# New due dates for a planned attention and feed-forward kernel, with odd-sized tiles moved into the pool of constants

## The chip, the core and the metric

The kernel runs on one core of a Trainium2 chip. The metric is the device time of one execution in microseconds. Three executions of the kernel before took 598.49, 599.57 and 600.98 us; their median, 599.57 us, is what the changed kernel is compared with.

## The reference

Local attention with a few global keys and a distance bias, and then a feed-forward block with a sigmoid gate. Batch 4, 8 heads, 768 positions, head width 64; 3,072 tokens of width 512 go through weights of 512 x 2048 and 2048 x 512.

```python
scores = scale * np.matmul(q, k.transpose(0, 1, 3, 2)) - slopes * dist   # 8 heads
scores = np.where(is_global | is_local, scores, -1000000000.0)           # 8 global keys, 96 local ones
a = np.exp(scores - np.max(scores, axis=-1, keepdims=True))
a = a / (np.sum(a, axis=-1, keepdims=True) + 1e-09)
x = np.matmul(a, v)                  # to (3072, 512)
h = x @ w_in                         # (3072, 2048)
out = (h * (1.0 / (1.0 + np.exp(-1.702 * h)))) @ w_out
```

## The kernel before

The work is cut into 24 blocks of 128 query rows and 12 chunks of two blocks. The four blocks that are the first of their batch are done in `first` with keys and queries turned by TensorE; every other block goes through `prep` (load of q, k and v into `raw`, split into two 16-bit halves, a transposing DMA into `QK`), four calls of `unit` (two heads each: `scores`, `rows` into a tile `p`, exponentials in place, halves into `hl`, a transposing DMA into `pt`, `values` into `pv`) and `finish` (weighing, halves into `x16`, a transposing DMA into `xT`). The weights are split in `weights` in 16 pieces. The feed-forward block of the first three chunks runs over eight steps each with `up` and `down`; from chunk 3 on `up_two` and `down_two` work on two steps at once with a scheme of seven products in place of eight.

Nothing is ordered by the compiler. Each piece of work is a `Task` with a cost in us for each engine that may run it (`on`), the tasks it waits for (`after`), the tiles it uses (`bufs`) and a wanted time. `Work.order` works out due dates backward along the dependences, adds to each task `NUDGE[tag]`, the correction that is written down for the name (`wk.tag`) of its piece, and then plays the plan through: an engine that is free takes, of the tasks that are ready and whose tiles are free, the one with the earliest due date. The instructions are emitted in that order, and each engine and the SP queue keep to it on the chip. A task isn't taken before `early()`, which is 24 us before its due date, or at `soon` where that is set. Pieces with the tag "" have no correction.

Nearly all DMAs are issued on SP's queue, in the plan's order: a DMA whose data isn't there yet holds up all that stand behind it. The plan charges a load of q, k or v 1.35 us, a transpose into `pt` 1.4 us, one into `QK` 2.8 us.

Tiles come from rings: `Ring` has a name, a number of buffers and whether its order is `loose`. `Buf()` gives the tile. `r_hl.tiles` are fixed tiles of the pool `const`; all others are allocated in the pool `sb` behind `const`, in the order of their first use. By the sizes in the code the tiles in `sb` of the kernel before begin between 64 and 416 bytes past a multiple of 512 bytes, and `hl` 416 bytes past one; none begins at a multiple. So `raw` and `t` stand at 160, `QK`, `VR` and `g` at 352, `x16` at 224.

Behind the main work stands a verdict on whether the fast way's assumptions held. Its inputs are sums and maxima that are gathered on the way (`checks`), among them second readings of the weights: 32 pieces `ws..again` of 512 KB that borrow the two buffers of the ring `wa`, each with one instruction of ScalarE (line 1024) and one of VectorE (line 1026), and of q, k and v of four blocks (`again`). The verdict has three tasks: `rows_hold` on VectorE, one small matmul (line 1072) on TensorE, and `all_hold` on VectorE, which writes `flag`. All engines then load `flag` and branch over the function `general`, a slow general version that isn't run here.

```python
    for c in range(2, NCHUNK):
        for s in range(NST):
            start[c, s] = t_
            t_ += PACE if c < TWO else PACE2
    v1 = add({"DVE": 2.4}, rows_hold, [covers, *checks])
    v2 = add({"PE": 0.1}, lambda e: nc.tensor.matmul(pb()[0:1, 0:3], ones, fin, start=True, stop=True), [v1], [pb])
    add({"DVE": 1.2}, all_hold, [v2], [pb], 575.0)
    redo = nc.values_load(flag[0:1, 0:1], min_val=0, max_val=1)
    with tc.If(redo > 0):
```

The last product of the kernel is piece `down113` (chunk 11, steps 6 and 7), wanted at `start[11, 6] + LAG`. With T0 = 20, 16 steps of 6 us, eight of 5.9 us (chunk 2) and 70 of 5.7 us, `start[11, 6]` is 562.2 us; LAG is 16, and the second half of the rows is wanted 2.6 us later. Its last output leaves by a DMA on ScalarE's queue (line 935).

Of the kernel before, what the change touches and what calls it, by code (L numbers as in the profile page):

```python
# [1 line left out]

# [6 lines left out]
F32 = mybir.dt.float32  # L9
F32R = mybir.dt.float32r  # L10
F16 = mybir.dt.float16
# [8 lines left out]
P = 128  # L20
NG = 32
# [5 lines left out]

NUDGE = {"T0": -15.8, "T1": -14.5, "T2": 7.5, "T3": 23.9, "block0": -14.5, "block1": -12.1, "block10": 7.2, "block11": 28.4,  # L30
# [27 lines left out]

NG = 8
SKIP = 24  # L60
# [18 lines left out]
        self.tiles = None  # L79


class Buf:


# [5 lines left out]

    def __call__(self):
        if self.ring.tiles:
            return self.view(self.ring.tiles[self.i % self.ring.bufs])
        if self.t is None:
            self.t = self.ring.pool.tile(self.shape, self.dtype, tag=self.ring.tag, name=self.name, bufs=self.ring.bufs)
        return self.t
# [14 lines left out]
class Work:  # L111
# [5 lines left out]
    def add(self, on, fn, after=(), bufs=(), want=1e9):  # L117
        t = Task(on, fn, [a for a in after if a is not None], bufs, want)
        t.tag = self.tag
        for a in t.after:  # L120
            a.next.append(t)
        for b in t.bufs:
            b.users.append(t)
        self.tasks.append(t)
        return t

    def order(self):
# [18 lines left out]
        for t in self.tasks:  # L146
            t.due += NUDGE.get(t.tag, 0.0)
        free = dict.fromkeys(("PE", "DVE", "ACT", "POOL", "SP"), 0.0)
# [84 lines left out]
def kernel(  # L233
# [12 lines left out]
    B, H, S, D = q.shape  # L246
# [11 lines left out]
    const = ctx.enter_context(tc.tile_pool(name="const", bufs=1))  # L258
# [31 lines left out]
    def ring(tag, bufs, pool=sb, loose=False):  # L290
        return Ring(pool, tag, bufs, loose, pool is ps)

    r_raw, r_qk16, r_QK, r_KG = ring("raw", 2), ring("qk16", 1), ring("QK", 3), ring("KG", 1)
    r_VR, r_VG, r_sm = ring("VR", 4), ring("VG", 1), ring("sm", 3)
    r_pr, r_hl, r_pt = ring("pr", 2), ring("hl", 2), ring("pt", 4)
    r_hl.tiles = [const.tile([P, 8 * P], F16, name=f"hl{j}") for j in range(2)]
    r_VF = ring("VF", 3, loose=True)
    r_x, r_x16, r_xT, r_xS = ring("x", 1), ring("x16", 1), ring("xT", 2), ring("xS", 2)
    r_ws, r_wa = ring("ws", 3), ring("wa", 2, loose=True)
    r_t, r_g = ring("t", 3, loose=True), ring("g", 3, loose=True)  # L300
# [5 lines left out]
    wk = Work()  # L306
# [115 lines left out]
    def load(n, raw, parts=(0, 1, 2)):  # L422
        b, i = place(n)
        return [add({"SP": 1.35}, lambda e, z=z: nc.sync.dma_start(
            raw()[:, z], (q, k, v)[z][b, :, i * P:(i + 1) * P, :].rearrange("h p d -> p h d")), bufs=[raw]) for z in parts]
# [525 lines left out]
    T0, PACE0, PACE, PACE2, LAG, SKEW, LEAD = 20.0, 6.0, 5.9, 5.7, 16.0, 3, 68.0  # L951
# [42 lines left out]
    whole = seq + [(c, s) for c in range(2, TWO) for s in range(NST)]  # L994
# [15 lines left out]
            down_two(c, S, start[c, 2 * S] + LAG)  # L1010
    wk.tag = ""
    for n in range(EARLY):
        raw = Buf(r_raw, [P, 3, H, D], F32, f"again{n}")
        ld = load(n, raw)
        guard(n, raw, ld, 440.0 + 30 * n)
        for t in ld:
            t.soon = 400.0 + 30 * n
    for s in range(NST):
        for u in range(2):
            for half in range(2):  # L1020
                ws = Buf(r_wa, [P, 512, 2], I32, f"ws{s}_{u}{half}again")
                t0 = add({"SP": 1.6}, lambda e, s=s, u=u, ws=ws, half=half: load_weights(nc, ws(), w_in, w_out, s, u, half), bufs=[ws])
                o, hi_w = 2 * (2 * s + u) + half, lambda ws=ws: ws()[:, :, 1].bitcast(F32)
                t1 = add({"ACT": 0.64}, lambda e, o=o, hi_w=hi_w: nc.scalar.activation(
                    hi_w(), hi_w(), AF.Square, accum_out=e2[:, 0, o:o + 1]), [t0], [ws])
                checks.append(add({"DVE": 0.6}, lambda e, o=o, hi_w=hi_w: nc.vector.tensor_reduce(
                    e2[:, 1, o:o + 1], hi_w(), axis=AX.X, op=ALU.min), [t1], [ws], 275.0 + 8.0 * o))
                t0.soon = 265.0 + 8.0 * o
# [9 lines left out]
    ones = const.tile([P, 1], F32, name="ones")  # L1038
    nc.gpsimd.memset(ones, 1.0)
    pb = Buf(r_h, [P, 512], F32, "pb")  # L1040

    def rows_hold(e):
        nc.vector.tensor_scalar(NM[:, 0:EARLY], top, 1.0 / SC, None, ALU.mult)
# [17 lines left out]
    def all_hold(e):  # L1061
# [6 lines left out]
            nc.vector.scalar_tensor_tensor(tot[:, 0:1], o_, 1.0, tot[:, 0:1], ALU.is_lt, ALU.add)  # L1068
        nc.vector.tensor_scalar(flag, tot[:, 0:1], 1.0, None, ALU.min)

    v1 = add({"DVE": 2.4}, rows_hold, [covers, *checks])
    v2 = add({"PE": 0.1}, lambda e: nc.tensor.matmul(pb()[0:1, 0:3], ones, fin, start=True, stop=True), [v1], [pb])
    add({"DVE": 1.2}, all_hold, [v2], [pb], 575.0)
# [215 lines left out]
```

## Time and profile before

| | before |
|---|---|
| median of 3 runs | 599.57 us (598.49 to 600.98) |
| profiled execution, its time | 598.66 us |
| its span, first to last instruction | 596.8 us |
| TensorE busy (matmuls) | 576.2 us, 97% |
| VectorE busy | 492.8 us, 83% |
| ScalarE busy | 460.4 us, 77% |
| granted TensorE clock, mean | 0.997 |
| SP's data queue, share of 16 engines' span | 87.8% |

Busy time of TensorE is the time in which a matmul was under way; its idle time is what is left of the span. The device time of the execution is 1.9 us longer than its span. Instructions of sequencers (loads of a register, branches, waits) don't count as busy.

### The profile page before, as it was taken

How to read it: one execution, taken by the hardware profiler on the slowest of the kernel's cores; microseconds unless marked ns; L12 is line 12 of the kernel's file. 1: busy time of each engine (PE TensorE's matmuls, PEld its weight loads, DVE VectorE, ACT ScalarE, POOL GpSimd, SP SyncE). 2: the span in 40 equal slices, each digit the busy share in tenths (PEclk: the TensorE clock that was granted, in tenths of full speed). 3: DMA queues.
4: the chain of work that ended last, by engine and by line, in shares of the span. 5: the costliest groups of instructions: out<-in, count | busy, mean ns of one | idle time of the engine just before them, and what ended most of it. 6: DMA issues, size and time to landing. Idle time of an engine off the chain costs nothing.

```text
span 596.8 us, 16959 instructions
## 1 busy us (share of the span) xinstructions
PE 576.2 (97%) x6774; PEld 432.5 (72%) x6776; DVE 492.8 (83%) x1164; ACT 460.4 (77%) x1091; POOL 1.6 (0%) x10
## 2 busy tenths in 40 slices
PE   8899999999999999999999999998999999999994
PEld 5787676777686668767677768767866875887893
DVE  5899999998999998887699889877969779776541
ACT  4688798998669888988579789858987897874441
POOL 1000000000000000000000000000000000000000
PEclk9999999999999999999999999999999999999998
DMA  8998999998996877799799999999998999971001
GB/s 223 315 307 242 269 233 243 190 201 171 177 153 118 151 152 162 146 186 204 170 230 197 199 197 190 222 191 192 217 222 197 210 202 174 251 143 36 20 1 41
DMA packets 268502, 109.58 MB, mean 184 GB/s; under 512 B 249536, under 2 KB 250048, under 8 KB 268416
## 3 DMA queue, kind: packets, MB, share of 16 engines
q1 hardware_dynamic: 267984, 108.30, 87.8%
q8 instruction: 54, 0.88, 0.7%
q14 instruction: 32, 0.26, 0.1%
q10 hardware_dynamic: 432, 0.13, 0.1%
HBM read 57.67 MB, written 6.29 MB: 107 GB/s over the span
## 4 chain that ended last, share of the span: by engine, by line
PE 58%; DVE 16%; DMA 10%; ACT 9%; issue 3%; SPq 2%; DVEq 0%; ACTq 0%
PE y L917 27%; PE pa L849 13%; PE pb L849 10%; PE s L556 3%; DMA raw<-in_q_dram 3%; ACT p L572 2%; DVE w L399 2%; DVE wa L396 2%; DMA ws_01again<-in_moe_w_in_dram 2%; DMA raw<-in_k_dram 2%; DMA QK<-QK 2%; DVE p L562 1%; ACT junk L431 1%; DVE hl L577 1%; PE h L809 1%
## 5 line engine op out<-in xcount | busy, mean ns | idle before, releaser
L917 PE MATMUL y<-w,g 128*128 128x512 f16 (+1 forms) x1248 | 265.1, 363 | 0.9 <-DVE g L890 0.9
L917 PEld LDWEIGHTS <-g 128*128 128x128 f16 x1248 | 118.0, 98 | 106.5 <-DVE g L890 1.4
L849 PEld LDWEIGHTS <-w 128*128 128x128 f16 x1728 | 100.8, 98 | 5.1 <-DVE t L882 0.7
L572 ACT ACTIVATE p<-p,NM 128x232 f32<-128x232 f32 x160 | 76.6, 481 | 9.2 <-DVE NM L562 9.0
L849 PEld LDWEIGHTS <-T 128*128 128x128 f16 x1296 | 76.8, 98 | 6.3 <-issue 0.8
L809 PE MATMUL h<-xT,w 128*128 128x256 f16 x576 | 68.3, 273 | 0.7 <-DVE t L819 0.7
L562 DVE CUSTOM_DVE_ANT_0 p<-s,mm 128x232 f32<-128x232 f32 x160 | 58.2, 395 | 6.0 <-PE s L556 4.9
L809 PEld LDWEIGHTS <-w 128*128 128x128 f16 x576 | 55.3, 98 | 9.4 <-issue 1.2
L577 DVE TENSOR_TENSOR hl<-p,hl 128x464 f16<-128x464 f32 x80 | 50.9, 637 | 11.2 <-ACT hl L576 10.9
L890 DVE SCALAR_TENSOR_TENSOR g<-t,g 128x512 f16<-128x512 f32 x72 | 48.9, 688 | 7.6 <-ACT g L889 7.1
L857 DVE TENSOR_TENSOR h<-pb,h 128x256 f32<-128x256 f32 x72 | 29.2, 419 | 26.6 <-PE pb L849 21.1
L889 ACT ACTIVATE g<-t 128x512 f16<-128x512 f32 x72 | 44.7, 627 | 7.4 <-DVE t L882 5.8
L881 ACT ACTIVATE t<-h 128x512 f32<-128x512 f32 (+1 forms) x72 | 36.3, 517 | 17.5 <-DVE h L857 15.9
L576 ACT CAST hl<-p 128x464 f16<-128x464 f32 x80 | 46.1, 576 | 3.6 <-DMA pt<-hl 2.0
L849 PE MATMUL pa<-xS,T 128*128 128x128 f16 x648 | 45.0, 220 | 0.7 <-ACT h L865 0.7
L882 DVE SCALAR_TENSOR_TENSOR t<-t,h 128x512 f32<-128x512 f32 x72 | 38.5, 553 | 5.9 <-ACT t L881 5.9
L556 PEld LDWEIGHTS <-QK 128*128 128x128 f16 x640 | 36.3, 98 | 6.9 <-DVE NM L562 2.1
L556 PE MATMUL s<-QK 128*128 128x128 f16 x320 | 38.5, 219 | 0.5 <-DMA QK<-QK 0.5
L849 PE MATMUL pb<-xS,w 128*128 128x128 f16 x540 | 37.2, 219 | 0.4 <-ACT h L854 0.4
L849 PE MATMUL pa<-xT,w 128*128 128x128 f16 x540 | 36.9, 220 | 0.5 <-DVE t L882 0.5
L587 PE MATMUL pv<-VR,pt 128*128 128x64 f16 x288 | 34.1, 194 | 2.6 <-DMA pt<-hl 2.6
L588 PE MATMUL pv<-VR,pt 128*128 128x64 f16 x288 | 34.1, 194 | 0.0
(178 smaller groups left out, 1004.3 us busy)
## 6 DMA issues: line engine op xcount, KB each, us to landing
ws<-in_moe_w_in_dram SPq DMA_DIRECT2D x8, 1024.0 KB
ws<-in_moe_w_out_dram SPq DMA_DIRECT2D x8, 1024.0 KB
raw<-in_q_dram SPq DMA_DIRECT2D x24, 256.0 KB
raw<-in_k_dram SPq DMA_DIRECT2D x24, 256.0 KB
out_dram<-yo SPq DMA_DIRECT2D x22, 256.0 KB
raw<-in_v_dram SPq DMA_DIRECT2D x20, 256.0 KB
QK<-QK SPq DMA_DIRECT2D x40, 128.0 KB
ws_00again<-in_moe_w_in_dram SPq DMA_DIRECT2D x8, 512.0 KB
```

Of the source, the lines that this page charges most:

```text
L556: nc.tensor.matmul(sp()[:, j, lo:hi], d["QK"]()[:, 0, h, :], K[:, 1 + z, h, P - (hi - lo):], start=(z == 0), stop=(z == 1), skip_group_che ...
L562: nc.vector.tensor_tensor_reduce(out=pr()[:, j, :], in0=sp()[:, j, :], in1=m, scale=-1.0 / SC, scalar=3.0e38, op0=ALU.add, op1=ALU.min, ac ...
L572: ex.append(add({"ACT": 0.473}, lambda e, j=j: nc.scalar.activation(pr()[:, j, :], pr()[:, j, :], AF.Exp, bias=NM[:, n, hs[j]:hs[j] + 1], ...
L576: t4 = add({"ACT": 0.5}, lambda e: nc.scalar.copy(hl()[:, 0, :, SKIP:], pr()), ex, [pr, hl])
L577: t5 = add({"DVE": 0.55}, lambda e: nc.vector.tensor_sub(hl()[:, 1, :, SKIP:], pr(), hl()[:, 0, :, SKIP:]), [t4], [pr, hl])
L809: nc.tensor.matmul(ph()[:, fi, :], w1(s, cc, z, fi), X[:, y, cc, :], start=(j + cc == 0), stop=(j == 2 and cc == NCC - 1))
L849: nc.tensor.matmul(o()[:, fi], w, x()[:, y * NCC + 2 * k + cc, t], start=(first and fi + j + cc == 0), stop=(last and j + cc == 3), skip_g ...
L881: t1 = add({"ACT": 0.06 + 0.22 * w}, lambda e: nc.scalar.activation(o(), src(), AF.Tanh, scale=0.851 / (SX * SW)), after, srcs)
L882: return add({"DVE": 0.08 + 0.265 * w}, lambda e: nc.vector.scalar_tensor_tensor(o(), o(), 1.0, src(), ALU.add, ALU.mult), [t1], srcs)
L889: t4 = add({"ACT": 0.53}, lambda e, g=g, tt=tt: nc.scalar.mul(g()[:, 0], tt(), SG / (SX * SW)), u, [tt, g])
L890: t5 = add({"DVE": 0.61}, lambda e, g=g, tt=tt: nc.vector.scalar_tensor_tensor(g()[:, 1], tt(), SG / (SX * SW), g()[:, 0], ALU.mult, ALU.s ...
L917: nc.tensor.matmul(y(), part(zg, f), w2(s, z, f % 2)[:, m], start=(begin and f + j == 0), stop=(end and j == 2 and f == 2 * len(steps) - 1 ...
```

## The change

It has three parts. The table of corrections is replaced: of 250 names in the two tables 248 have another value, half of them by 8 us or more and 67 by more than 20 us. The second readings (`twice0` to `twice31`, `again0` to `again3`) and the verdict get names, and with them corrections of their own. And the tiles of the rings `VF`, `sm`, `pr` and `KG`, whose sizes are no multiples of 512 bytes, are taken out of `sb` and fixed in `const`, with two unused tiles (`gap0`, 96 bytes, and `gap1`, 192 bytes) as padding; `Buf()` cuts the wanted shape out of them with `whole`. By the sizes in the code `hl` and every tile of `sb` then begin at a multiple of 512 bytes; `VF`, `sm`, `pr`, `KG` and `mm` don't all.

```diff
...
-         "down100": 3.6, "down101": -5.5, "down102": 18.8, "down103": 7.3, "down11": -20.3, "down111": 2.6, "down112": 1.3,
-         "down113": -136.5, "down12": -26, "down13": -0.2, "down14": -33, "down15": 34.8, "down16": -59.9, "down17": -13.1,
...
+NUDGE = {"T0": 2.5, "T1": 0.8, "T2": 8.3, "T3": 19, "again1": -2.1, "again2": -15.5, "again3": 3, "block0": -140.3, "block1":
...
+         "down110": -1.4, "down111": -1.8, "down112": -3.5, "down113": 13.3, "down12": -9.9, "down13": 0.6, "down14": -128.9,
...
+         "twice0": 3.4, "twice1": -5.7, "twice10": 10.8, "twice11": -4.5, "twice12": -5.9, "twice13": 15.2, "twice14": -61.2,
...
+         "up110": -1.7, "up111": -1, "up112": 0.3, "up113": -5.2, "up12": 7.2, "up14": -2.2, "up15": 2.8, "up16": 8.6,
...
+         "up91": 5.9, "up92": -29.8, "up93": -10, "verdict": -4.6, "w00": -12, "w01": -3, "w10": 9.7, "w20": -99.3, "w21":
...
+def whole(t, shape):
+
+    a = t[0:shape[0], 0:prod(shape[1:])]
+    if len(shape) == 2:
+        return a
+    names = "abcd"[:len(shape) - 1]
+    return a.rearrange(f"p ({' '.join(names)}) -> p {' '.join(names)}", **dict(zip(names[1:], shape[2:])))
...
-            return self.view(self.ring.tiles[self.i % self.ring.bufs])
+            t = self.ring.tiles[(self.ring.taken.index(self) if self.ring.loose else self.i) % self.ring.bufs]
+            return self.view(t) if self.view else whole(t, self.shape)
...
+    const.tile([P, 24], F32, name="gap0")
     r_hl.tiles = [const.tile([P, 8 * P], F16, name=f"hl{j}") for j in range(2)]
     r_VF = ring("VF", 3, loose=True)
+    for r, elements, dtype in ((r_VF, H * (D + 1), F32), (r_sm, 2 * H, F32), (r_pr, 4 * P - 2 * SKIP, F32), (r_KG, 2 * H * NG, F16)):
+        r.tiles = [const.tile([P, elements], dtype, name=f"{r.tag}{j}") for j in range(r.bufs)]
...
+        wk.tag = f"again{n}"
...
+                wk.tag = f"twice{2 * (2 * s + u) + half}"
...
+    const.tile([P, 48], F32, name="gap1")
...
+    wk.tag = "verdict"
     v1 = add({"DVE": 2.4}, rows_hold, [covers, *checks])
```

## Rows read from the trace of the kernel before

**Rows 1.** The page: busy time by engine, and the chain's shares.

```profile
PE 576.2 (97%) x6774; PEld 432.5 (72%) x6776; DVE 492.8 (83%) x1164; ACT 460.4 (77%) x1091; POOL 1.6 (0%) x10
...
PE 58%; DVE 16%; DMA 10%; ACT 9%; issue 3%; SPq 2%; DVEq 0%; ACTq 0%
```

**Rows 2.** Windows: length, busy us (instructions) by engine, clock, DMA share, GB/s.

```profile
0.00:50.00 50.00, 45.32 (x421) 34.45 (x424) 41.07 (x90) 34.05 (x52) 1.58 (x10) 1.00 0.99 284
50.00:525.00 475.00, 467.33 (x5600) 345.52 (x5598) 416.86 (x989) 397.35 (x975) 0.00 (x0) 1.00 0.98 195
525.00:575.00 50.00, 50.00 (x612) 40.39 (x610) 29.89 (x71) 24.49 (x54) 0.00 (x0) 1.00 0.21 47
575.00:596.80 21.80, 13.53 (x151) 12.14 (x148) 5.01 (x16) 4.53 (x11) 0.00 (x0) 0.93 0.09 28
```

**Rows 3.** TensorE's waits, 50 to 575 us: total, times, longest.

```profile
PE pv L587 <- DMA pt<-hl: 2.6, 3, 1.7
...
PE y L917 <- DVE g L890: 0.9, 1, 0.9
...
PE s L556 <- DMA QK<-QK: 0.5, 1, 0.5
```

**Rows 4.** The page: DMA packets, and the queue that carries them.

```profile
DMA packets 268502, 109.58 MB, mean 184 GB/s; under 512 B 249536, under 2 KB 250048, under 8 KB 268416
...
q1 hardware_dynamic: 267984, 108.30, 87.8%
```

**Rows 5.** Chain piece (start, us), and the window of the longest stall.

```profile
399.55 5.51 DMA pt<-hl
...
402.00:406.00 4.00, 2.31 (x38) 1.78 (x37) 2.69 (x6) 3.53 (x11) 0.00 (x0) 1.00 1.19 197
```

**Rows 6.** The chain in the first 25 us: start, us, what.

```profile
1.27 5.46 DMA raw<-in_k_dram
...
9.44 8.97 DMA raw<-in_q_dram
```

**Rows 7.** Groups by shape: count, busy us, mean ns, idle before.

```profile
L890 DVE SCALAR_TENSOR_TENSOR g<-t,g 128x512 f16<-128x512 f32 x72 | 48.9, 688 | 7.6 <-ACT g L889 7.1
...
L721 DVE TENSOR_TENSOR x<-x,x 128x512 f16<-128x512 f32 x20 | 13.7, 686 | 0.5 <-ACT x L719 0.2
```

**Rows 8.** Second readings, one of four tiles: min/median/max ns, first and last start.

```profile
L229 SPq DMA_DIRECT2D ws_01again<-in_moe_w_in_dram x8: 381/552/1392, 275.4 to 506.9; - x8
L1024 ACT ACTIVATE ws_01again<-ws_01again x8: 664/682/690, 281.9 to 521.8; 128x512 f32<-128x512 f32 x8
```

**Rows 9.** Timeline of VectorE: the last instruction of the verdict's first task.

```profile
557.93 0.22 DVE L1059 TENSOR_REDUCE fin<-swt 128x1 f32<-128x8 f32 x2
```

**Rows 10.** Timeline of the end: start, us, engine, line, tiles [idle before].

```profile
580.39 8.02 PE L917 MATMUL y<-w,g 128*128 128x256 f16 x72
...
588.34 0.19 PE L1072 MATMUL pb<-fin,ones 128*1 128x3 f32 x2
588.45 0.38 ACT L930 ACTIVATE yo<-y 128x256 f32<-128x256 f32 x1 [2.18 <-PE y L917]
...
588.86 0.36 ACTq L935 DMA_DIRECT2D out_dram<-yo  x1
...
589.72 0.14 DVE L1069 TENSOR_SCALAR flag<-tot 1x1 int32<-1x1 f32 x1
```

**Rows 11.** Sequencers behind the verdict: min/median/max ns, first to last start.

```profile
L1088 ACTq TENSOR_LOAD <-flag x1: 468/468/468, 589.9 to 589.9; - x1
...
L1089 SPq EVENT_SEMAPHORE  x8: 17/17/17, 594.5 to 595.1; - x8
L1089 ACTq COMPARE_BRANCH  x1: 54/54/54, 590.4 to 590.4; - x1
...
L1089 ACTq EVENT_SEMAPHORE  x1: 17/17/17, 594.3 to 594.3; - x1
...
L1284 SPq EVENT_SEMAPHORE  x10: 17/28/28, 595.1 to 596.8; - x10
```

More of the change, by code (lines that the diff above doesn't have):

```diff
@@ L1 @@
 from contextlib import ExitStack
+from math import prod
 import concourse.bass as bass
@@ L26 @@
 LOW = 1e8
-NUDGE = {"T0": -15.8, "T1": -14.5, "T2": 7.5, "T3": 23.9, "block0": -14.5, "block1": -12.1, "block10": 7.2, "block11": 28.4,
[27 rows of a table removed]
+NUDGE = {"T0": 2.5, "T1": 0.8, "T2": 8.3, "T3": 19, "again1": -2.1, "again2": -15.5, "again3": 3, "block0": -140.3, "block1":
[31 rows of a table added]
 NG = 8
```

52 rows, old and new, of the table NUDGE are left out of this document.

## The prediction

> **What bounds the kernel now.** I read the page first: TensorE is busy 97% of the span, and the chain that ended last runs through TensorE for 58% of it, through VectorE for 16% and through DMAs for 10% [rows 1]. A share of busy time can hide where the time is to be had, so I asked next for windows. The reader is to subtract TensorE's busy time from the length of each [rows 2]: 4.7 us idle in the first 50 us, 7.7 us from 50 to 525, nothing from 525 to 575, and 8.3 us in the last 21.8. That is 20.7 us in all. The granted clock is 1.00 in every window before the last, so the matmuls themselves give nothing back: the change adds and removes no product, and 576.2 us of TensorE stay. What the change can move is these 20.7 us, and what it can add is more of them.
>
> Then the waits. Of the 7.7 us in the middle, 2.6 and 0.5 us ended with a DMA, the transposes into `pt` and the copies in `QK`; the other 4.6 us ended with an instruction of VectorE or ScalarE, the longest listed 0.9 us [rows 3]. The same windows show the DMA engines at a share of 0.98 from 50 to 525 us and 0.99 before that, against 0.21 afterwards, where TensorE has no idle time [rows 2]. One queue carries 87.8% of the 16 engines' span, nearly all of it in packets under 512 bytes [rows 4]. The worst place shows what late transfers cost: the transpose issued at 399.55 us lies on the chain for 5.51 us, and TensorE idles 1.7 of the 4 us from 402 to 406 [rows 5].
>
> **The end, step by step.** The last group of 72 products ends at 580.39 + 8.02 = 588.41 us; the verdict's matmul comes behind it at 588.34, and `flag` is ready at 589.72 + 0.14 = 589.86 [rows 10]. But its input has been complete since 557.93 + 0.22 = 558.15 us [rows 9]. So the verdict waits 30 us for TensorE, and the reason stands in the dates: it is due at 575 - 1.2 - 0.2 = 573.6, while `down113` is due at 562.2 + 16 - 136.5 = 441.7 (444.3 for its second half), so the plan takes the products first. In the new table `down113` is due at 591.5 and 594.1 and the verdict at 569.0. The order turns round: the matmul goes ahead of the last products, and `all_hold` fits behind it while they run.
>
> What that gives: ScalarE's last DMA is issued by 588.86 + 0.36 = 589.22 [rows 10], but its load of `flag` starts at 589.9 [rows 11], so 0.64 us of ScalarE's path go. The branch at 590.4 is followed by 3.8 us until ScalarE's next wait at 594.3, the same for SP, whose list of waits starts only at 594.5 and takes 595.1 - 594.5 plus about 0.5 us more, 1.1 us, up to the last ten [rows 11]. With `flag` early, SP would have passed the branch and stand in its list when ScalarE arrives. Sum: 0.64 + 1.1 = 1.75 us less. The bounds are 0 (the matmul stays last) and 1.75; I take 1.75, as both dates are read from the tables. What the moved work costs: 0.19 us of TensorE, which it pays today too [rows 10], and eight small instructions of VectorE behind it, from 588.34 + 0.19 = 588.53 to 589.86, 1.3 us. If they stand before the last gate's multiplication they delay it by that much; VectorE has 16.8 of 21.8 us idle in this window [rows 2], so I count nothing, 1.3 us where that cover is gone.
>
> **The addresses.** Engines: the gate's product on tiles that start 160 and 352 bytes past a multiple of 512 takes 688 ns, and the subtraction on tiles at 160 and 224 takes 686 ns with the same 512 columns [rows 7]; I count nothing for VectorE and ScalarE. DMAs: no tile of the kernel before begins at a multiple of 512, so the trace can't price it. Below, nothing. Above, all that ends with a DMA: 3.1 us of waits in the middle [rows 3], and in the first 50 us at most the 4.7 us of idle time [rows 2], where two loads of `raw` of 5.46 and 8.97 us stand on the chain [rows 6]. I take 2.0 us of the 3.1 and 0.5 of the 4.7: the chain's DMA pieces are long against what TensorE loses by them, so that a transfer shortened by a fifth frees much of the loss, and the first loads must be waited for at any address.
>
> The queue's 87.8% of 596.8 us is 524 us on each engine, over 268,502 packets, so 31 ns a packet on average [rows 4], and 93% of the packets are under 512 bytes. [...]
>
> **The dates.** The second readings keep their work: 32 times one ScalarE instruction of 0.68 us, one VectorE instruction about as long, and a DMA whose issue takes 0.55 us of SP [rows 8]. Their corrections move them against the rest on three engines and past SP's queue of loads and transposes, and the other corrections reorder everything. No row tells what a new order does to TensorE's 4.6 us of waits on VectorE and ScalarE. Bounds: all of them go (-4.6), or as much again comes on top (+4.6). I take -0.5. Nothing in the table touches the number of products or transfers.
>
> **The sum.** 1.75 + 2.0 + 0.5 + 0.5 = 4.75 us less than the profiled execution's 598.66, so 593.9. The median of the runs shown is 0.9 us above that execution, so I say **594.8 us**.
>
> **The rivals.**
> - *The DMAs become light.* All 3.1 us of DMA-ended waits go, half of the 4.7 us at the start, and half of the 4.6, since VectorE's and ScalarE's inputs come by DMA as well: 1.75 + 3.1 + 2.35 + 2.3 = 9.5 us less, 590.0 us as a median. For it: a DMA share of 0.98 wherever TensorE idles [rows 2]. Against it: more of the idle time ends with VectorE and ScalarE than with a DMA [rows 3]. [...] Chance 0.15.
> - *Only the end moves.* The addresses do nothing, and the new order stalls as often as the old: 597.8 us; 599.6 if the verdict's matmul isn't taken early after all, and the change so doesn't do what it says. For it: no row shows an address that matters, and 7.7 us in 475 is already little. Chance 0.27.
> - *A second reading gets in the way.* SP's queue keeps the order of issue, so a second reading, or a block's load, dated far earlier than today holds the DMA engines and a buffer of `wa` ahead of a transpose into `pt`. The price of one such place is seen at 402 to 406 us, 1.7 us [rows 5]. To end up slower by 0.5% it takes 3.0 us and what the end gives, 4.75 us: three more such places than now decide it. With four, 599.6 - 1.75 + 6.8 = 604.6 us. For it: 67 corrections moved by more than 20 us, and a DMA share that leaves no room [rows 2]. Against it: these readings are spread from 275 to 522 us today [rows 8], and only few stalls end with a DMA [rows 3]. Chance 0.13.
>
> **How the numbers follow.** My forecast has a chance of 0.45, the rivals 0.15, 0.27 and 0.13. A difference under 0.5%, 3.0 us, is about what a measurement of this kernel can't tell from none; faster is then below 596.6. The forecast's own range is 592 to 597, the light DMAs lie below it, and the second rival just above. Faster: 0.45 and 0.15, from which little is taken for the forecast's upper edge and given back by the second rival's lower one, 0.60. Same: 0.27. Slower: 0.13. The range: down to 588.5, the light DMAs with 1.5 us more of the start, and up to 601.5, which leaves out the dear cases of the third rival.
>
> **What would show it.** In the changed kernel's profile: line 1072's matmul before the last group of products, and `flag` written before 588; the time from the last product to the span's end 6.6 us in place of 8.4. DMA share under 0.95 and a share of the queue below 85% if the addresses count, and unchanged if they don't. TensorE idle about 5 us from 50 to 525. It is wrong if that idle time is 10 us or more, or if the start loses more than 6.

## The result and the profile after

The changed kernel takes 592.15 us (590.42 to 595.13, five executions) against 599.57 us for the kernel before (598.49 to 602.42, five): a ratio of 0.9867, interval 0.9822 to 0.9911, so about 8.0 us less by the ratio and 7.4 by the two medians, where 4.75 us less had been forecast. On another chip the same kernel came out at 0.9833 (0.9787 to 0.9879), 10 us less. The profiled execution took 590.42 us, with a span of 588.6 us; it is the shortest of the five.

The page of the changed kernel: busy time, the chain's shares, and the queue that carries nearly all packets.

```profile
PE 575.0 (98%) x6774; PEld 432.7 (74%) x6776; DVE 495.8 (84%) x1166; ACT 458.8 (78%) x1089; POOL 1.6 (0%) x10
...
q1 hardware_dynamic: 267984, 108.30, 81.7%
...
PE 86%; DMA 6%; DVE 4%; issue 1%; ACT 1%; SPq 1%; POOL 0%; DVEq 0%; POOLq 0%
```

The chain has moved from VectorE and the DMAs to TensorE, 86% where it was 58% [rows 1], and the queue's share fell from 87.8% [rows 4] to 81.7% with the same packets and bytes. The windows of the changed kernel, columns as in [rows 2]:

```profile
0.00:50.00 50.00, 45.34 (x426) 34.86 (x429) 41.42 (x91) 33.85 (x52) 1.58 (x10) 1.00 0.95 286
50.00:525.00 475.00, 471.21 (x5691) 350.44 (x5689) 424.47 (x1000) 400.68 (x985) 0.00 (x0) 1.00 0.91 196
525.00:575.00 50.00, 50.00 (x585) 40.27 (x584) 26.80 (x66) 21.21 (x49) 0.00 (x0) 1.00 0.10 26
575.00:588.60 13.60, 8.42 (x81) 7.11 (x77) 3.08 (x12) 3.04 (x7) 0.00 (x0) 0.92 0.14 45
```

Subtracting TensorE's busy time from each length gives 4.7, 3.8, 0 and 5.2 us idle, 13.6 in all, where the kernel before had 4.7, 7.7, 0 and 8.3, 20.7 [rows 2]. So 7.0 us of idle time went, and 1.2 us of busy time, which makes the 8.2 us between the two spans. Nothing came from the start; 3.9 us came from the middle and 3.1 from the end.

TensorE's waits in the changed kernel from 50 to 575 us, with the columns of [rows 3] (total, times, longest):

```profile
PE pv L605 <- DMA pt<-hl: 2.0, 2, 1.7
PE s L574 <- DMA QK<-QK: 0.7, 1, 0.7
PE h L827 <- DVE t L837: 0.6, 1, 0.6
PE s L574 <- DVE NM L580: 0.4, 1, 0.4
```

The waits that end with a DMA are 2.7 us, hardly less than the 3.1 of [rows 3]. Those that end with VectorE or ScalarE fell from 4.6 to 1.0 us. That isn't how the prediction had it, and the experiments take it up.

The end. First the last pieces of the changed kernel's chain (start, us, what), then its sequencers (ns as minimum, median and maximum, first and last start):

```profile
575.34 2.62 PE y L935 x24
577.96 0.12 PE pb L1094 x2
578.08 5.36 PE y L935 x48
```

```profile
L1110 ACTq TENSOR_LOAD <-flag x1: 476/476/476, 584.3 to 584.3; - x1
...
L1111 SPq EVENT_SEMAPHORE  x8: 17/17/17, 585.8 to 586.3; - x8
...
L1111 DVEq COMPARE_BRANCH  x1: 72/72/72, 580.1 to 580.1; - x1
...
L1111 SPq COMPARE_BRANCH  x1: 58/58/58, 583.0 to 583.0; - x1
L1111 DVEq EVENT_SEMAPHORE  x1: 21/21/21, 583.4 to 583.4; - x1
...
L1111 ACTq COMPARE_BRANCH  x1: 54/54/54, 584.8 to 584.8; - x1
L1111 ACTq EVENT_SEMAPHORE  x1: 17/17/17, 587.3 to 587.3; - x1
...
L1306 SPq EVENT_SEMAPHORE  x10: 17/28/548, 586.4 to 588.5; - x10
```

The verdict's matmul (L1094) now stands ahead of the last 48 products, VectorE and SP branch while these run, and only ScalarE's branch is left behind them. From the last product (578.08 + 5.36 = 583.44) to the end of the span it is 5.2 us, 8.4 before [rows 2, 10].

### The profile page after: what moved, and what is told of

The parts are those of the page before. It is cut to its first block, busy times and chain, and to the rows that moved or that the text cites. A ratio compares the mean times of both kernels' runs of the same rounds, so it can differ in the third digit from the quotient of the medians.

```text
span 588.6 us, 16939 instructions
## 1 busy us (share of the span) xinstructions
PE 575.0 (98%) x6774; PEld 432.7 (74%) x6776; DVE 495.8 (84%) x1166; ACT 458.8 (78%) x1089; POOL 1.6 (0%) x10
## 3 DMA queue, kind: packets, MB, share of 16 engines
q1 hardware_dynamic: 267984, 108.30, 81.7%
## 4 chain that ended last, share of the span: by engine, by line
PE 86%; DMA 6%; DVE 4%; issue 1%; ACT 1%; SPq 1%; POOL 0%; DVEq 0%; POOLq 0%
PE y L935 38%; PE pa L867 16%; PE pb L867 12%; PE h L827 8%; PE s L574 5%; DMA pt<-hl 2%; DMA VF<-in_v_dram 2%; DMA QK<-QK 2%; PE pv L605 1%; PE pv L607 1%; PE pv L606 1%; DMA ws<-in_moe_w_out_dram 1%; PE idle L1100 1%; DVE w L417 1%; PE pv L672 1%
## 5 line engine op out<-in xcount | busy, mean ns | idle before, releaser
L590 ACT ACTIVATE pr<-pr,NM 128x232 f32<-128x232 f32 x160 | 76.6, 480 | 8.5 <-DVE NM L580 8.0
L580 DVE CUSTOM_DVE_ANT_0 pr<-s,mm 128x232 f32<-128x232 f32 x160 | 58.1, 393 | 7.4 <-PE s L574 5.6
L595 DVE TENSOR_TENSOR hl<-pr,hl 128x464 f16<-128x464 f32 x80 | 50.8, 636 | 6.7 <-ACT hl L594 6.1
L594 ACT CAST hl<-pr 128x464 f16<-128x464 f32 x80 | 45.8, 575 | 6.8 <-DMA pt<-hl 5.5
L899 ACT ACTIVATE t<-VF 128x512 f32<-128x512 f32 (+1 forms) x72 | 36.3, 517 | 17.5 <-DVE VF L875 16.8
L875 DVE TENSOR_TENSOR VF<-pb,VF 128x256 f32<-128x256 f32 x72 | 29.4, 419 | 22.6 <-PE pb L867 18.6
L900 DVE SCALAR_TENSOR_TENSOR t<-t,VF 128x512 f32<-128x512 f32 (+1 forms) x72 | 38.7, 551 | 4.8 <-ACT t L899 4.5
```

The lines of the kernel that those rows point to most:

```text
L580: nc.vector.tensor_tensor_reduce(out=pr()[:, j, :], in0=sp()[:, j, :], in1=m, scale=-1.0 / SC, scalar=3.0e38, op0=ALU.add, op1=ALU.min, ac ...
L590: ex.append(add({"ACT": 0.473}, lambda e, j=j: nc.scalar.activation(pr()[:, j, :], pr()[:, j, :], AF.Exp, bias=NM[:, n, hs[j]:hs[j] + 1], ...
L594: t4 = add({"ACT": 0.5}, lambda e: nc.scalar.copy(hl()[:, 0, :, SKIP:], pr()), ex, [pr, hl])
L595: t5 = add({"DVE": 0.55}, lambda e: nc.vector.tensor_sub(hl()[:, 1, :, SKIP:], pr(), hl()[:, 0, :, SKIP:]), [t4], [pr, hl])
```

## The experiments

Each ratio is to the kernel before on the same chip. Its median there was 603.38 us for the four runs of the first part, 603.99 for the changed kernel again, the shifts by 160 and by 256 and the dates taken out, and 600.18 for the two shifts of `hl` or `sb` alone, the dates put in and the branch. The us gained or lost are worked out from the ratio; the two medians give values up to about 1 us away from them. "Idle in the middle" is TensorE's, 475 us less its busy time from 50 to 525 us; it comes from one profiled execution, while the ratio comes from all. The changed kernel itself gave 3.8 and 5.2 us in two executions, so one us there decides nothing.

### The three parts by themselves

**The addresses alone.** The new tiles, with the old table and no new names. The edit against the changed kernel (most of the table is not shown):

```diff
-NUDGE = {"T0": 2.5, "T1": 0.8, ...
+NUDGE = {"T0": -15.8, "T1": -14.5, ...
-        wk.tag = f"again{n}"
-                wk.tag = f"twice{2 * (2 * s + u) + half}"
-    wk.tag = "verdict"
```

> The new addresses with the old table and without the new names. Three theories share the 7.4 us that the change gained. Mine, that the parts add: the end has 3.3 us (5.2 us from the last product to the end of the span in place of 8.4), the addresses 2 to 2.5, the dates the rest; then this kernel takes about 597.3 us, SP's queue falls from 87.8% to 82 to 83%, and TensorE idles 5 to 6 us from 50 to 525 where it idled 7.7. Rival one, the dates do it all: 599.6 us, idle time as before, whatever the queue does. Rival two, the addresses do all that the end doesn't: about 595.5 us and under 4.5 us of idle time there.

Measured: 599.79 us, ratio 0.993 (0.9892 to 0.9967), 4.2 us less. The queue stands at 81.3%. The profiled execution, at 602.28 us, was one of the dearer ones: 10.5 us idle in the middle, where 5 to 6 had been expected, 4.1 of them in one wait for `pt`. The addresses are worth something without the new dates, and the end isn't in it (8.6 us).

**The dates alone.** The new table and the new names, with the tiles where they were. The edit against the kernel before (most of the table is not shown):

```diff
-NUDGE = {"T0": -15.8, "T1": -14.5, ...
+NUDGE = {"T0": 2.5, "T1": 0.8, ...
+        wk.tag = f"again{n}"
+                wk.tag = f"twice{2 * (2 * s + u) + half}"
+    wk.tag = "verdict"
```

> The new table and names with the old addresses. If the parts add: 594.5 us, SP's queue near 88%, the end as short as in the changed kernel, TensorE idle 5 to 6 us from 50 to 525. If the dates do it all: 592 us and under 4.5 us of idle time. If the addresses do all but the end: 596.3 us and 7 us or more of idle time.

Measured: 596.35 us, ratio 0.988 (0.9843 to 0.9918), 7.2 us less, with 5.1 us from the last product to the end and 6.9 us idle in the middle. Its queue, one window, and its waits:

```profile
q1 hardware_dynamic: 267984, 108.30, 87.9%
```

```profile
50.00:525.00 475.00, 468.05 (x5582) 346.27 (x5581) 419.93 (x991) 396.57 (x973) 0.00 (x0) 1.00 0.97 193
```

```profile
PE pv L591 <- DMA pt<-hl: 4.0, 3, 2.1
PE h L813 <- DVE t L823: 0.9, 1, 0.9
PE s L560 <- DMA QK<-QK: 0.9, 1, 0.9
```

The queue is as full as before. The waits on VectorE and ScalarE are 475 - 468.05 - 4.9 = 2.1 us, 4.6 before, and the waits on DMAs 4.9, 3.1 before [rows 3]: the new order takes waits off the engines and leaves some of them at the DMAs. With the new addresses on top the DMA waits are 2.7 us.

**The verdict ahead, nothing else.** The kernel before with two corrections of the new table (the rest of the table is not shown):

```diff
-NUDGE = {"T0": -15.8, ... "down113": -136.5, ...
+NUDGE = {"verdict": -4.6, "T0": -15.8, ... "down113": 13.3, ...
+    wk.tag = "verdict"
```

> The kernel before with only the last products dated later and the verdict 4.6 us earlier, as in the new table. If the end gained because the branches of ScalarE, VectorE and SP no longer fall together: 5.2 us from the last product to the end, 3.3 us less, 596.3 us. If only the waits in series are saved, as the prediction summed them: 6.6 us, 597.8 us. Nothing before 540 us differs in either.

Measured: 600.04 us, ratio 0.9945 (0.9914 to 0.9976), 3.3 us less; from the last product to the end 5.2 us, and 8.3 us idle in the middle. ScalarE's branch in this kernel:

```profile
L1090 ACTq COMPARE_BRANCH  x1: 54/54/54, 593.0 to 593.0; - x1
L1090 ACTq EVENT_SEMAPHORE  x1: 17/17/17, 595.5 to 595.5; - x1
```

**The verdict last again.** The changed kernel with one correction raised:

```diff
-"verdict": -4.6,
+"verdict": 40,
```

> The changed kernel with the verdict dated 44.6 us later, so that its matmul comes behind all products. If the three branches falling together is what costs: 8.4 us from the last product to the end, and about 3.8 us from each branch to the next instruction; 595.4 us. If the short end came from elsewhere in the change: under 6.7 us, 593.7 us or less.

Measured: 597.51 us, ratio 0.9907 (0.9872 to 0.9942), 5.6 us less, the end 8.5 us. Its branches:

```profile
L1111 SPq EVENT_SEMAPHORE  x8: 17/17/17, 593.7 to 594.2; - x8
L1111 ACTq COMPARE_BRANCH  x1: 54/54/54, 589.4 to 589.4; - x1
...
L1111 DVEq COMPARE_BRANCH  x1: 72/72/72, 589.5 to 589.5; - x1
L1111 SPq COMPARE_BRANCH  x1: 58/58/58, 589.7 to 589.7; - x1
...
L1111 ACTq EVENT_SEMAPHORE  x1: 17/17/17, 593.5 to 593.5; - x1
L1111 DVEq EVENT_SEMAPHORE  x1: 21/21/21, 593.5 to 593.5; - x1
```

From the last product to the end, the order of the verdict is worth 8.4 - 5.2 = 3.2 us in the old table and 8.5 - 5.2 = 3.3 in the new one. The three engines branch within 0.3 us of each other here and are all held for 4.0 to 4.1 us; ScalarE, branching 1.8 us behind SP with the verdict ahead, is held for 2.5. That the engines slow one another here is how these traces read; no run moves one engine's branch alone.

### What in the addresses

**The changed kernel again**, unchanged, to stand beside the next ones.

> The changed kernel itself, once more, so that the three beside it are compared with it on one chip. Either theory: a ratio near 0.987 to the kernel before, 5.2 us from the last product to the end, SP's queue near 82%.

Measured: 593.54 us, ratio 0.9833 (0.9787 to 0.9879), queue 82.6%, 5.2 us idle in the middle.

**Shifted by 160 bytes**, `hl`, the odd-sized tiles and all of `sb`. The instructions stand in the same order on every engine:

```diff
-    const.tile([P, 24], F32, name="gap0")
+    const.tile([P, 64], F32, name="gap0")
```

> The changed kernel with 160 bytes more in front of hl, so that hl and all tiles of the main pool begin 160 bytes past a multiple of 512; the order of every engine is the same. If the addresses still count when the new order is there: SP's queue goes back to about 88%, the waits for transposes grow, and the time is 2 to 4 us above the changed kernel's, a ratio of 0.990 to 0.994 to the kernel before. If the new order alone hides the transfers: queue near 88% too, but a time within 1 us of the changed kernel's, 0.987.

Measured: 595.59 us, ratio 0.9878 (0.983 to 0.9926), queue 87.6%, 6.5 us idle in the middle.

**Shifted by 256 bytes**, the same tiles:

```diff
-    const.tile([P, 24], F32, name="gap0")
+    const.tile([P, 88], F32, name="gap0")
```

> The same with 256 bytes in place of 160, again with the same order. If what costs is a packet that crosses a multiple of 256 bytes: queue near 82% and the changed kernel's time. If a multiple of 512 is needed: queue near 88% and the time of the shift by 160.

Measured: 593.32 us, ratio 0.9826 (0.9781 to 0.987), queue 82.7%, 4.8 us idle in the middle. The queue of the changed kernel again, of the shift by 160 and of the shift by 256:

```profile
q1 hardware_dynamic: 267984, 108.30, 82.6%
q1 hardware_dynamic: 267984, 108.30, 87.6%
q1 hardware_dynamic: 267984, 108.30, 82.7%
```

So 256 bytes past a multiple of 512 does as well as a multiple, and 160 bytes past one brings back the whole of the queue's share. In time the shift by 160 costs 0.0045 of 604 us, 2.7 us (2.1 by the medians), which the two intervals don't settle by themselves; five of the six executions of the changed kernel are below all six of the shifted one.

**Only `hl`, or only `sb`, shifted by 160.** In the first the padding behind is made smaller by as much, so `hl` and the odd-sized tiles move and `sb` stays; in the second `sb` moves and all in front of it stays:

```diff
-    const.tile([P, 24], F32, name="gap0")
+    const.tile([P, 24 + 40], F32, name="gap0")
-    const.tile([P, 48], F32, name="gap1")
+    const.tile([P, 48 - 40], F32, name="gap1")
```

> The changed kernel, the two hl tiles alone begin 160 bytes past a multiple of 512; everything else, and the order on each engine, stays. If the addresses count where the transposes into pt read, the queue is back at 85 to 88% and the time 1 to 2.7 us above the changed kernel's, about 0.986 to 0.988 of the kernel before. If they count in the other tiles, queue 82 to 83% and 0.983 as before on such a chip.

```diff
-    const.tile([P, 48], F32, name="gap1")
+    const.tile([P, 48 + 40], F32, name="gap1")
```

> The changed kernel, all tiles but the two of hl begin 160 bytes past where they do; the order on each engine stays. The counterpart of the last: if hl alone counts, queue 82 to 83% and 0.983 of the kernel before; if the other tiles count, queue 85 to 88% and 0.986 to 0.988. If both count, the two kernels share the rise of the queue from 82 to 88% between them.

Measured: 590.61 us, 0.9841 (0.9816 to 0.9867) with `hl` shifted, and 594.73 us, 0.991 (0.9879 to 0.9941) with `sb` shifted. The queue of the first and of the second:

```profile
q1 hardware_dynamic: 267984, 108.30, 82.7%
```

```profile
q1 hardware_dynamic: 267984, 108.30, 86.9%
```

These two intervals lie apart; the ratios differ by 4.1 us. It is the tiles of `sb` whose place counts: `raw`, `QK`, `pt`, `xT`, the weights. The place from which the 80 transposes into `pt` read (`hl`) doesn't show.

Which tile of `sb` it is was not tried, but the traces answer a part of it. In the first 50 us SP issues nothing but loads of q, k, v and the weights; the first transpose follows at 52.7 to 54.5 us. That window in the changed kernel again, with `hl` shifted and with `sb` shifted:

```profile
0.00:50.00 50.00, 45.50 (x429) 35.21 (x432) 41.46 (x91) 33.93 (x52) 1.58 (x10) 1.00 0.94 284
0.00:50.00 50.00, 45.88 (x431) 35.21 (x432) 41.36 (x91) 34.06 (x52) 1.59 (x10) 1.00 0.93 284
0.00:50.00 50.00, 44.21 (x417) 33.84 (x418) 39.69 (x88) 33.44 (x51) 1.58 (x10) 1.00 0.94 271
```

About the same DMA share moves 284 GB/s in the first two and 271 in the third, so a byte costs about 5% more DMA time with `sb` off its place, before any transposing DMA. Loads into `sb` have their part in the price; what the transposes add to it stays open.

### What in the dates

**The second readings' dates taken out** of the changed kernel, all else left:

```diff
-        wk.tag = f"again{n}"
-                wk.tag = f"twice{2 * (2 * s + u) + half}"
```

> The changed kernel with the second readings back under the empty name, so without corrections of their own, and all else as in the change. If their own dates carry what the new table gains besides the end: 3 to 4 us above the changed kernel, a ratio near 0.993. If the other corrections carry it, or the transfers have room enough: within 1 us, 0.987 to 0.989. The table was made with them, so a mixed order may also be slower than its parts; then TensorE's idle time from 50 to 525 us rises above 8 us.

Measured: 603.58 us, ratio 0.9998 (0.9969 to 1.0026), 10 us above the changed kernel on the same chip. It is idle for 9.9 us in the middle and 3.4 more from 525 to 575 us. It has the end and the addresses of the changed kernel, so its mixed order must cost about as much as these two give. The three longest groups of its waits from 50 to 575 us:

```profile
PE pv L605 <- DMA pt<-hl: 4.1, 4, 2.2
PE pb L867 <- ACT xS L762: 2.4, 1, 2.4
PE pb L867 <- ACT VF L872: 2.1, 4, 0.8
```

**The second readings' dates put in** by themselves, into the kernel before (its last line stands ahead of the verdict):

```diff
-NUDGE = {"T0": -15.8, ...
+NUDGE = {"again1": -2.1, ... "twice9": 12.1, "T0": -15.8, ...
+        wk.tag = f"again{n}"
+                wk.tag = f"twice{2 * (2 * s + u) + half}"
+    wk.tag = ""
```

> The kernel before, with the names and the corrections of the second readings alone; every other correction, the addresses and the verdict's date stay as before. The new table with its own end gave 0.988 of the kernel before, and the end alone 0.9945, so about 3.9 us came from the order of the other work. If the readings' dates carry that gain by themselves, this kernel stands at about 0.992 to 0.995, with the verdict still last and 8.4 us behind the last product. If the gain belongs to the table as a whole, the readings are placed against an order that they were not made for: 1.00 or more, TensorE idle 8 us or more from 50 to 525 us. Queue 88% by either.

Measured: 605.29 us, ratio 1.0082 (1.0053 to 1.0112), 4.9 us slower, with 8.9 us idle in the middle and 50 - 48.78 = 1.2 us from 525 to 575. TensorE's waits on DMAs are short here, 0.4 us in all for `pt`; the longest groups end with ScalarE and VectorE. So neither the readings' dates nor the others bring anything without their counterpart. The gain of the dates is that of one order as a whole, and no share of it can be given to the readings.

### What in the end

**The general version out of the branch.** The kernel before, in which `general`, which is jumped over, gives way to four small instructions on four engines; its order and its addresses stay:

```diff
     with tc.If(redo > 0):
-        general(ctx, tc, q, k, v, ng, nl, w_in, w_out, out)
+        nc.vector.memset(wok, 0.0)
+        nc.scalar.mul(tot, tot, 1.0)
+        nc.gpsimd.memset(fin, 0.0)
+        nc.sync.dma_start(out[0:1, 0:2], wok)
```

> The kernel before, with four small instructions, one on each of four engines, in the branch in place of the general version (which is left out: it would run only if the flag were set, and it isn't). Order, dates and addresses stay. If the 3.8 us behind each engine's branch are the jump over the general version's long code, they shrink to under 1.5 us and the last product is 5 to 6 us before the end of the span in place of 8.4: 0.994 to 0.996 of the kernel before. If the branch itself costs them, whatever it jumps over, 8.4 us and 1.000.

Measured: 596.72 us, ratio 0.9939 (0.9916 to 0.9962), 3.7 us less, with 4.3 us from the last product to the end where 5 to 6 had been expected. Its sequencers at the branch, and its queues of the kind instruction:

```profile
L1089 ACTq COMPARE_BRANCH  x1: 54/54/54, 590.8 to 590.8; - x1
...
L1089 SPq COMPARE_BRANCH  x1: 54/54/54, 590.8 to 590.8; - x1
...
L1089 ACTq EVENT_SEMAPHORE  x1: 17/17/17, 591.0 to 591.0; - x1
...
L1089 SPq EVENT_SEMAPHORE  x1: 17/17/17, 591.0 to 591.0; - x1
...
L1287 SPq EVENT_SEMAPHORE  x10: 17/28/28, 591.4 to 593.1; - x10
```

```profile
q8 instruction: 53, 0.87, 0.6%
q14 instruction: 26, 0.21, 0.1%
```

The hold of 3.9 us on ScalarE and 3.7 on SP behind the branch [rows 11] is 0.2 us here: it is the jump over the general version's code, not the branch or the load of `flag`. The two queues carry 79 packets where the kernel before has 54 + 32 = 86; that the missing ones are code brought in for the jump would fit, and is not shown. SP has one wait at the branch in place of eight, so 0.6 us of the gain is that shorter list (594.5 to 595.1 in [rows 11]), which is why the end came out shorter than expected. The branch's own record is 54 to 72 ns on ScalarE, SP and VectorE, with the short jump's 0.2 us as with the long jump's 2.5 to 4.1 us.

## Why the prediction was right, and where its sizes were off

The range held the time, and the end, the addresses in the middle and the dates all gave time, as forecast; the start, put at 0.5 us, gave nothing. The sum was too small: 592.15 us is 2.65 below the 594.8 of the forecast, and the 4.75 us forecast are less than the 5.3 that the interval allows at least. That the time lies in the range owes as much to its width, 588.5 to 601.5, as to the sum. Two sizes were wrong, and one was about right for a reason that is shown only in part.

**The end: 3.3 us, not 1.75.** The order turned round as the two dates said, and the terms that the prediction had are there. ScalarE's load of `flag` follows its last DMA at once, as the 0.64 us assumed. From ScalarE's first wait behind the branch to the end of the span it is 588.6 - 587.3 = 1.3 us, where it was 596.8 - 594.3 = 2.5 [rows 11]: 1.2 us for SP's list, 1.1 predicted. Of that 1.1 the rows show 0.6, the eight waits from 594.5 to 595.1, behind which the ten begin at once [rows 11]; the other 0.5 stood in no row, and came true because SP in the changed kernel is past the first of its ten (586.4) when ScalarE arrives (587.3). What failed is that the hold behind the branch was taken as fixed. It went from 590.4 to 594.3, 3.9 us [rows 11], to 584.8 to 587.3, 2.5 us, now that VectorE and SP branch earlier: another 1.4. Then 0.64 + 1.2 + 1.4 = 3.2 us. The 1.3 us that `all_hold` could have cost on VectorE isn't seen: the verdict ahead by itself gained 3.3.

**The addresses: near the 2.5 us forecast, or somewhat more.** Measured were 4.2 us with the old order, 2.7 (not settled by itself) and 4.1 us with the new one. The 0.5 us at the start didn't come: TensorE idles 4.7 us there before and after. Nothing for the engines was right: the gate's product takes 685 ns where it took 688 [rows 7]. The prediction looked for the other 2.0 us in the DMA-ended waits of the kernel before. Against that kernel these fell by only 0.4 us, since the new order had by itself raised them to 4.9; from there to 2.7 is 2.2 us. That is from one execution each. With the new order `pt` alone stands at 2.0, 3.7, 2.7 and 2.8 us in the four executions with `sb` in place (the changed kernel twice, the shift by 256, `hl` shifted), and at 4.0, 4.1 and 3.2 in the three with `sb` off it; so that a transfer shortened by the addresses is what frees TensorE there is likely, and not shown for each of the waits. The queue's part is shown: from 0.878 x 596.8 = 524 us on each engine to 0.817 x 588.6 = 481, so 43 us, or 31.3 to 28.7 ns a packet; on one chip and in one order it is 0.876 x 593.5 = 520 against 0.826 x 590.5 = 488, 32 us. So a transfer became 6 to 8% shorter. The fifth that the prediction assumed, on which its 2.0 us rest, is shown by no run; these 6 to 8%, and 2.2 us less of waits, stand in its place. The direction is shown, and the shift by 256 bytes, which costs nothing (82.7% against 82.6%), shows that a multiple of 512 isn't needed. Why tiles at 160 bytes past one cost the queue and tiles at 256 don't, no run here tells.

**The dates: about 3.9 us, not 0.5.** The dates alone gave 7.2 us, the verdict ahead alone 3.3; the rest, 0.0065 of 603 us, has an error of about 0.0049 (the two half-widths, 0.0038 and 0.0031, squared and added), so 3.9 us with 3.0 either way. The bound of 4.6 us holds the 3.9, but not the whole of its error; the value was put near zero for want of a row, so this term was a guess and its sign luck. In the waits it is seen as 4.6 us behind VectorE and ScalarE that became 2.1 with the dates alone and 1.0 with both.

The terms together, 3.3 + 3.9 + 2.7 to 4.2, are 9.9 to 11.4 us; the whole gave 8.0 and 10.1 us on two chips. They add up within the errors, and overlap a little: the verdict last again, which has the dates and the addresses without the end, gave 5.6 us, where 3.9 and 2.7 to 4.2 make 6.6 to 8.1.

**What the sum left out: the clock.** The prediction took TensorE's 576.2 us as fixed, since the granted clock is 1.00 up to the last window [rows 2]. Two windows of the dates alone, behind the wait of 2.11 us that ended at 343.2 us, and one of the addresses alone, around the end of the wait of 4.10 us at 101.1, show another price of a wait:

```profile
340.00:345.00 5.00, 2.58 (x45) 2.24 (x43) 3.43 (x13) 3.78 (x11) 0.00 (x0) 0.94 1.03 189
345.00:350.00 5.00, 5.00 (x34) 3.24 (x32) 4.12 (x10) 4.07 (x11) 0.00 (x0) 0.72 0.61 131
```

```profile
100.00:105.00 5.00, 3.89 (x37) 2.24 (x38) 3.62 (x8) 3.85 (x9) 0.00 (x0) 0.66 1.15 291
```

What is missing to 1.00 makes (0.06 + 0.28) x 5 = 1.7 us in the one and 0.34 x 5 = 1.7 in the other, and it stands in the profile as busy time. The profiled executions of the kernel before and of the changed one have no such stretch up to the last product. So of the 6.4 us between the spans of the dates alone and the changed kernel 2.9 are idle time and 3.5 busy time, 1.7 of them from the clock. Of the kernel before's 41 executions on the first two of the three chips, 17 with a mean clock of 0.994 or less took 602.0 to 608.1 us and 24 with 0.995 or more 598.8 to 605.0; the changed kernel stood at 0.997 to 1.000 in all of its eleven. (The mean counts also the last few us, in which TensorE has no work; in the kernel before the clock is 0.50 from 594 to 596 us.) A part of the gain is likely the clock's; no run parts it from the rest.

**The rivals.** The light DMAs forecast 590.0 us, and on the second chip the ratio times 599.57 is 589.6; but their condition, that no wait on a DMA is left, fell: 2.0 and 3.7 us for `pt` stay, and the gain came as much from the end and the order. That only the end moves is refuted by the addresses alone and the dates alone. That a second reading gets in the way fits both mixed tables: with the readings' dates put in, 4.9 us above the kernel before, and with them taken out, 10 us above the changed kernel; in the table as a whole it doesn't happen. The way that was described isn't shown: with the dates put in, TensorE's own waits end with ScalarE and VectorE, and whether a transfer that SP's queue holds up stands behind these was not followed.

**The marks.** The matmul ahead of the last products, the DMA share under 0.95 (0.91), the queue under 85% (81.7%) and about 5 us idle in the middle (3.8 and 5.2) came as written, as did a start that loses no more than 6 us (4.7); 6.6 us from the last product to the end came as 5.2.

## What to carry to other kernels

Where a DMA queue is full and its packets are small (87.8% and mostly under 512 bytes here [rows 4]), work out where the tiles that it reads and writes begin: here some padding that put them at multiples of 256 bytes took 4.2 to 6.5 points off the queue's share and 2.7 to 4.2 us off the time, with the order of the instructions unchanged. Work that only the end needs, and a branch above all, belongs ahead of the last products and not behind them (3.2 to 3.3 us here), and code that is never run is best not put between a branch and the end (3.7 us here). A table of dates that was made as a whole is measured as a whole: here one part of it by itself gave +4.9 us, the rest without that part 0, and the whole with the addresses -8 to -10. And idle time isn't the whole price of a wait: look at the granted clock of the few us behind it, which made 1.7 us more of one wait of 2.1 us and of one of 4.1 here.

## What had not been expected of the hardware

- A branch over long code held ScalarE, VectorE and SP for 3.7 to 4.1 us when the three took it within 0.4 us of each other, ScalarE for 2.5 us when it took it 1.8 us behind SP, and each for about 0.2 us when the code was short. With the verdict last, TensorE and GpSimd were held for 0.4 to 0.5 us by the same long jump, which no run here explains.
- Behind a wait of 2.1 us TensorE's granted clock was 0.94 and 0.72 in two windows of 5 us, and around the end of one of 4.1 us 0.66 in one window of 5 us; what is missing to 1.00 is 1.7 us each time, on top of the wait.
- Tiles that begin 160 bytes past a multiple of 512 cost the queue as much as the old mixture of places (87.6% and 87.8%), tiles 256 bytes past one cost nothing (82.7% against 82.6%). Loads into tiles at 160 bytes pay a part of it (271 GB/s against 284 in the first 50 us, at about the same DMA share), the tile that the transposes into `pt` read from doesn't (82.7%).
